# First routing of a two-layer expert kernel: another layout of the list values, and another order of the work around it

## The chip, the cores and the metric

One core of one Trainium2 chip runs the whole program. The metric is the device time of one execution in microseconds (us). Besides TensorE (PE; PEld is its weight load), VectorE (DVE), ScalarE (ACT) and GpSimd (POOL), SP issues most of the DMAs, and POOL issues the gathers and scatters.

## The reference

The input goes through a 2-D Fourier transform (real part), then through a first layer of 8 experts weighted by a Sinkhorn iteration over all tokens, then through a second layer in which each token goes to one expert only:

```
X = fft(fft(x, axis=1), axis=2).real            # x: 8 x 3072 x 256
x = X.reshape(24576, 256)
logits = x @ w_gate;  logits -= logits.max()
P = exp(logits)
for _ in range(8):
    P /= P.sum(1, keepdims=True) + 1e-9
    P /= P.sum(0, keepdims=True) + 1e-9
    P *= N / E
out = sum over e of P[:, e:e+1] * (relu(x @ w1[e]) @ w2[e])          # first layer
# second layer: logits = out @ w_gate2, the row's best expert alone, scaled by its softmax weight
```

The exponentials of the first layer are zero for most rows and experts, so only the few rows that count are routed to experts.

## The kernel before

**Stages.** The transform writes rows to a DRAM table `H` and logits to an SBUF tile `L`. Then `route1` finds which rows and experts matter, and makes for each of `NT1` = 29 tiles (128 rows each: three per expert for 8 experts, and five "free" ones) the list of rows. `moe1` gathers those rows from `H`, builds inputs from them (`build`, four steps a to d), turns them with TensorE transposes (`turn`) and runs the experts one after the other. `route2` and `moe2` do the same for the second layer. The order of instructions on each engine is the order of the program text; work that belongs beside other work is put in by hand through `hooks` and `Slots` (a slot is a place between the groups of matmuls of an expert).

**The list products (`route1`).** Each partition holds `NSA` = 64 slots. `oh` (29 tiles x 64 slots, bf16) marks the tile of each slot, `bv` holds two values per tile and slot (`v` = 0: the row's column `ja`; `v` = 1: the partition's number), and `ah` marks the row within the tile (128 rows x n slots, made by `rows` in the chunks `CH1` = 24, 24 and 16). `put` then issues one matmul per slot, 64 in all, which add up in one PSUM tile `pl`: weights `ah[:, :, i]` (128 x 128, elements 48 or 32 bytes apart) and values `bv[:, :, :, a + i]` (58 columns, 128 bytes apart, since the slot is the innermost dimension of `bv`). From `pl` DVE works out `j`, and from that `R["hidx"]`, the rows to gather; then `signs` prepares further masks and a second product (`bq`, 24 matmuls of 16 columns with the first chunk's `ah`) into a tile of the pool `py`.

**What fills the engines meanwhile.** `G2` is a string for each hook of `route1`: `g` is one half of an expert's small weight product (`gates2`, half-gate; 16 matmul records with `wg2`), `0` to `3` make the high part (`part`) of a piece of expert 0's weights on ACT and put its low part (a DVE subtraction) on a list, `l` and `z` issue DMAs (a copy of `L`, zero fills of `out` and `acc`), `w` is one matmul of zeros (`warm`). `hooks[3]` comes between `bv` and the matmuls of `put`, `hooks[4]` behind them: there `low(0)` runs both low parts of expert 0's w1 on DVE and then fetches the next weights. After the first two groups of gathers, `fill(5)` issues the last half-gates.

**Weight loads.** `FETCH` is the order of the loads and their buffers: `("t", 7, "a")` is the last expert's transposed w2, which the half-gates of expert 7 need. It goes to buffer `rawa`, which expert 0's w1 occupies until `low(0)` is done. Buffers "1" and "2" are tiles of the pools that hold the experts' split weights. `gates2` fetches the next load behind experts 0, 1, 2 and 7.

**Into expert 0.** In `moe1`, `build(0, V, i)` makes the three input tiles of expert 0 on DVE as their gathers land; `moe.turn` transposes them in six matmuls, with a hook behind each pair that issues two 512-column matmuls of zeros (`lambda i: warm(2)`) from the pool `py`, which has two buffers; then the first layer's matmuls (`ph`) begin. `rest[3]` in slot (0, 0) runs the two low parts of expert 0's w2.

Of the kernel before, what the change touches and what calls it, by code (L numbers as in the profile page):

```python
# [7 lines left out]
F32 = mybir.dt.float32  # L8
F32R = mybir.dt.float32r
BF16 = mybir.dt.bfloat16  # L10
# [8 lines left out]
HW = 281  # L19
# [542 lines left out]


def route1(nc, rt, L, rmx, K, R, keep, pool, ring, hooks):
    o = rt.o
# [92 lines left out]
    oh = rt.tiles(T, tb, NSA)  # L658
    bv = T([2, NT1, NSA], BF16, name="bv")
    o.tt(bv[:, 0], oh, ja[:, None, :].to_broadcast([128, NT1, NSA]), ALU.mult)  # L660
    nc.scalar.activation(out=bv[:, 1, :, :NSL], in_=oh[:, :, :NSL], func=AF.Copy, scale=C("p"))
    nc.scalar.activation(out=bv[:, 1, :, NSL:], in_=oh[:, :, NSL:], func=AF.Copy, scale=C("p128"))
    hooks[3]()
# [3 lines left out]
    for n in CH1:  # L667
        a = NSL if a is None else a % NSA
        ah = rt.rows(ring, rb, a, n)
        late = late or ah  # L670
        rt.put(pl, ah, bv, a, n, a == NSL, a + n == NSL)
        a += n
    eq, gq = T([8, NSL], name="eq"), T([8], name="gq")
    o.tt(eq, ja[:, NSL:NSL + 8, None].to_broadcast([128, 8, NSL]), ja[:, None, :NSL].to_broadcast([128, 8, NSL]), ALU.is_equal)
    o.tt(eq, eq, gp[:, None, :NSL].to_broadcast([128, 8, NSL]), ALU.mult)
    hooks[4]()
    lst, li = S([2, NT1], name="lst"), T([NT1], I32, name="li")
# [10 lines left out]
    def signs():  # L688
# [8 lines left out]
        o.stt(R["ow"], R["hidx"], 2.0, sb, ALU.mult, ALU.add)  # L697

        o.red(gq, eq, ALU.add)
        tq, rq, _ = rt.split(T, gq, None, 8, "q")  # L700
# [334 lines left out]
def dense(tc, ctx, A, K, rt, R, Ld, H, Pd, out, wg2):  # L1035
# [69 lines left out]
    with tc.For_i(0, NT, 1) as i:  # L1105
# [17 lines left out]
        for s in range(2):  # L1123
# [26 lines left out]
FETCH = [("t", 0, "a"), ("t", 1, "b"), ("t", 2, "c"), ("t", 3, "1"), ("t", 4, "2"), ("t", 5, "2"), ("w1", 0, "a"), ("w2", 0, "b"),  # L1150
         ("t", 6, "c"), ("t", 7, "a"), ("w1", 1, "a"), ("w2", 1, "b")]
FETCH += [(w, e, b) for e in range(2, E) for w, b in (("w1", "a"), ("w2", "b"))]
# [4 lines left out]
def run(tc, ctx, A, out, H, acc, Ld, Pd, Gd, Zd):  # L1157
# [62 lines left out]
    with tc.manual_schedule():  # L1220
# [27 lines left out]
        with ExitStack() as st:  # L1248
# [7 lines left out]
            def gates2(e, qs=(0, 1)):  # L1256
# [15 lines left out]
                raw.pop(("t", e))  # L1272
                if e < 3 or e == E - 1:
                    fetch()
# [24 lines left out]
            with ExitStack() as s1:  # L1299
# [15 lines left out]
                def fill(k):  # L1315

                    def f():
                        for c in G2[k]:
# [5 lines left out]
                            elif c == "z":  # L1324
# [4 lines left out]
                                for a in range(0, n, 512):  # L1329
                                    w = min(512, n - a)  # L1330
                                    nc.sync.dma_start(out=av[:, a:a + w], in_=zt[:, 0, :w])
                            elif c == "w":
                                warm(1)
                            else:
                                part("w", 0, int(c), nc.vector, lows[int(c) // 2])
# [3 lines left out]
                def low(k):  # L1339
                    for f in lows[k]:  # L1340
                        f()

                signs, later = route1(nc, rt, L, rmx, K, R, S, r1, ring, [fill(i) for i in range(1, 5)] + [lambda: low(0)])
                X = {}

# [18 lines left out]
            with ExitStack() as s1:  # L1364
# [16 lines left out]

                turned, more = moe1(nc, K, R, rt, lg, hot, acc, moe, W, part, X, xg, Gd, *rows("w1", "w2"), xb, pt, zeros, zt, later[:2] + (rest, lambda: low(1), grab), ask, rt.C("tro"), lambda i: warm(2), lambda: xg.tile([128, CAP, HW], F32, name="Xg").rearrange("p a b -> p (a b)")[:8, :512])
            with ExitStack() as s1:
# [92 lines left out]
BACK, BF, BL = [(8,), (8,), (8,), (8,), (4, 8), (2, 4, 6, 8)], ((2, 9), (4, 9), (6, 9)), 8  # L1476
G2 = ("gg", "", "gggggg", "0lz12g3gg", "ggww", "ggg")
Y2 = (2, 3, 9, 10)
# [114 lines left out]
def moe1(nc, K, R, rt, lg, hot, acc, moe, W, part, X, xg, Gd, w1f, w2f, xb, pt, zeros, zt, rest, ask, trash, warm, grow):  # L1593
# [116 lines left out]
    for i in range(CAP):  # L1710
        for f in build(0, V, i):
            f()
    xt = moe.turn(lambda i: x[0][:, i], warm)
    for i, f in zip((0, 1, 3, 4), (rest[3], rest[0], rest[1], begin)):
        sl.at(0, i, f)
# [146 lines left out]
```

## Time and profile before

| | |
|---|---|
| median of 3 runs | 662.18 us (656.67, 662.18, 663.15) |
| profiled execution, its own time | 660.44 us |
| its span, first to last instruction | 658.7 us |
| mean granted TensorE clock | 0.97 |
| PE busy | 627.1 us (95%), 4794 matmuls |
| PEld busy | 600.1 us (91%) |
| DVE busy | 442.6 us (67%) |
| ACT busy | 321.6 us (49%) |
| POOL busy | 194.6 us (30%) |

All rows come from this one execution; times are us from the start of its span. The routing and the way into expert 0 lie between 197 and 249 us. Matmuls are pipelined, so a busy PE there is not PE at its peak: the spacing of the instructions and the granted clock say more.

### The profile page before, as it was taken

To read this page: it belongs to the slowest core of one execution; us is meant where nothing else is said; L and a number is where in the kernel's file an instruction comes from. 1 tells how busy PE (TensorE), PEld (TensorE's weight loads), DVE (VectorE), ACT (ScalarE), POOL (GpSimd) and SP (SyncE) were. 2 spreads that over 40 slices of the span, in tenths; PEclk is the share of its full clock that TensorE was granted. 3 is DMA by queue.
4 is the path that set the end of the run, shared out by engine and by line. 5 is a ranking of instruction groups with operands and counts; after the bars stand their busy time and mean duration, and the time that the engine had idled before them with its cause. 6 is when DMAs were issued, how large, how long until landed. Compare 5 with 4: busy or idle time off the path is not lost. (4 is left out here: it accounts for less than half of the span.)

```text
span 658.7 us, 12655 instructions
## 1 busy us (share of the span) xinstructions
PE 627.1 (95%) x4794; PEld 600.1 (91%) x4794; DVE 442.6 (67%) x1019; ACT 321.6 (49%) x717; POOL 194.6 (30%) x325
## 2 busy tenths in 40 slices
PE   9999999999998989999999998997999999999985
PEld 6899999999998968999999988984899999999984
DVE  4697787777238948659898789664555664674570
ACT  3455555555544204657556555531455564574441
POOL 0002221022110078831201102123686654431331
PEclk9999999999999879999999999998899999999988
DMA  8999999999979765676766758992565547635500
GB/s 222 285 234 323 279 274 280 260 301 308 343 256 374 300 192 177 199 269 206 258 206 218 281 179 229 307 374 44 176 214 194 205 148 296 237 138 210 208 33 29
DMA packets 56785, 152.58 MB, mean 232 GB/s; under 512 B 8292, under 2 KB 25836, under 8 KB 49165
## 3 DMA queue, kind: packets, MB, share of 16 engines
q1 hardware_dynamic: 47500, 114.69, 54.4%
q0 software_dynamic: 8752, 36.50, 17.0%
q8 instruction: 40, 0.66, 0.4%
q10 hardware_dynamic: 464, 0.51, 0.2%
q14 instruction: 29, 0.23, 0.1%
HBM read 101.50 MB, written 50.07 MB: 230 GB/s over the span
## 5 line engine op out<-in xcount | busy, mean ns | idle before, releaser
L933 PE MATMUL py<-w2h,hh 128*128 128x256 f32 (+1 forms) x472 | 137.0, 290 | 1.4 <-ACT y L1655 1.4
L436 DVE SCALAR_TENSOR_TENSOR hl<-ph,hh 128x384 fp32r<-128x384 f32 (+1 forms) x161 | 84.6, 542 | 78.1 <-ACT hh L886 75.8
L933 PE MATMUL py<-w2l,hh 128*128 128x256 f32 (+1 forms) x472 | 134.5, 285 | 2.3 <-DVE w2l L836 2.0
L933 PE MATMUL py<-w2h,hl 128*128 128x256 f32 (+1 forms) x472 | 134.9, 286 | 1.3 <-DVE hl L436 1.0
L886 ACT ACTIVATE hh<-ph 128x384 fp32r<-128x384 f32 (+1 forms) x161 | 75.8, 481 | 60.4 <-PE ph L900 32.7
L933 PEld LDWEIGHTS py<-w2l,hh 128*128 128x128 f32 x472 | 90.3, 191 | 2.7 <-DVE w2l L836 2.2
L933 PEld LDWEIGHTS py<-w2h,hl 128*128 128x128 f32 x472 | 90.1, 191 | 2.1 <-DVE hl L436 1.6
L933 PEld LDWEIGHTS py<-w2h,hh 128*128 128x128 f32 x472 | 90.1, 191 | 1.8 <-ACT y L1655 1.6
L900 PE MATMUL ph<-xh,w1h 128*128 128x384 f32 x256 | 68.2, 348 | 4.3 <-DVE hl L436 3.8
L900 PE MATMUL ph<-xh,w1l 128*128 128x384 f32 x256 | 65.3, 336 | 0.0
L900 PE MATMUL ph<-xl,w1h 128*128 128x384 f32 x256 | 65.3, 336 | 0.0
L74 PE MATMUL pp<-ca,w 96*128 96x96 f32 x512 | 59.0, 275 | 0.0
L74 PEld LDWEIGHTS pp<-ca,w 96*128 96x128 f32 x512 | 58.2, 192 | 0.5 <-ACT Z L97 0.2
L807 POOL DMA_INDIRECT out_dram<-y,Rorow x30 | 31.8, 1062 | 89.5 <-ACT hh L886 37.8
L126 POOL TENSOR_TENSOR lc<-hd 128x32 f32<-128x32 f32 (+1 forms) x25 | 9.5, 380 | 164.4 <-ACT hd L122 149.4
L900 PEld LDWEIGHTS ph<-xh,w1h 128*128 128x128 f32 x256 | 45.0, 189 | 7.6 <-DVE hl L436 6.0
L84 DVE COPY t<-pp 128x512 f32<-128x512 f32 (+2 forms) x56 | 33.3, 608 | 24.2 <-PE pp L82 24.2
L91 PE MATMUL pp<-cb,t 128*128 128x128 f32 x368 | 47.5, 276 | 0.6 <-DVE t L84 0.6
L900 PEld LDWEIGHTS ph<-xh,w1l 128*128 128x128 f32 x256 | 46.5, 189 | 0.0
L900 PEld LDWEIGHTS ph<-xl,w1h 128*128 128x128 f32 x256 | 46.3, 188 | 0.0
L76 ACT ACTIVATE at<-pp 128x384 f32<-128x384 f32 x64 | 31.1, 491 | 30.6 <-PE pp L74 30.1
L91 PEld LDWEIGHTS pp<-cb,t 128*128 128x128 f32 x368 | 44.4, 192 | 0.9 <-DVE t L84 0.8
(346 smaller groups left out, 1262.9 us busy)
## 6 DMA issues: line engine op xcount, KB each, us to landing
out_dram<-zt SPq DMA_DIRECT2D x48, 512.0 KB
H<-hd SPq DMA_DIRECT2D x24, 562.0 KB
xa<-in_xa_dram SPq DMA_DIRECT2D x32, 384.0 KB
xm<-in_xm_dram SPq DMA_DIRECT2D x32, 384.0 KB
rawa<-in_w_dram SPq DMA_DIRECT2D x8, 1024.0 KB
rawb<-in_w_dram SPq DMA_DIRECT2D x8, 1024.0 KB
rawa<-in_u_dram SPq DMA_DIRECT2D x8, 1024.0 KB
rawb<-in_u_dram SPq DMA_DIRECT2D x8, 1024.0 KB
```

The costliest lines, as they stand in the source:

```text
L74: nc.tensor.matmul(p[:M, i], lhs(4 * h + i), ca, start=True, stop=True)
L76: nc.scalar.activation(out=at[:M, :, :, s0:s0 + 4], in_=p[:M].rearrange("m s g j -> m g j s"), func=AF.Copy)
L84: nc.vector.tensor_copy(out=t[:, :n, :M], in_=p[:, :n, :M])
L91: nc.tensor.matmul(p[:M, i * 128:(i + 1) * 128], t[:, i, :M], cb[:, (g0 + i) * 128:(g0 + i + 1) * 128], start=True, stop=True)
L126: nc.gpsimd.tensor_tensor(out=lc[:np_, :n], in0=hd[:np_, :, 129:137], in1=hd[:np_, :, 273:281], op=ALU.add)
L436: self.nc.vector.scalar_tensor_tensor(out, a, s, b, op0, op1)
L807: nc.gpsimd.indirect_dma_start(out=dst, out_offset=bass.IndirectOffsetOnAxis(ap=idx, axis=0), in_=src, in_offset=None, **kw)
L886: self.nc.scalar.activation(out=a[:, :n], in_=p[:, :n], func=AF.Relu)
L900: self.nc.tensor.matmul(p[:, :N], w, xx, start=(i == 0), stop=(i == 5))
L933: self.nc.tensor.matmul(p[:, :nd], c, W[2 + m // 4][w][:, m % 4, :nd], start=(m == 0 and i == 0), stop=(m == 7 and i == 2))
```

## The change

- `bv` is laid slot by slot: for each slot its 58 values stand side by side. DVE and ACT write it through a transposed view. A new function `packed` takes the place of `put` for the first product: the 58 values of a slot are read contiguously and streamed twice (116 columns; the second copy lands in columns of `pl` that nobody reads).
- Expert 7's w2 (`t`, 7) goes to a buffer of pool "1" and is fetched behind expert 3's half-gates, not behind `low(0)`.
- `G2`: one half-gate moves ahead of the positions, one ahead of the products; the two zero matmuls `ww` become five `v`, each of two 512-column matmuls of zeros in the pool `ph`.
- `low(0)` at `hooks[4]` runs only its first low part; the second, and the fetch behind it, run after the builds of expert 0, before `turn`. The two `eq` operations move from before `hooks[4]` into `signs`.
- `turn` no longer gets matmuls of zeros in its hook.

```diff
+    def packed(self, pl, ah, bv, a, n, first, last):
+        nv = bv.shape[2]
+        for i in range(n):
+            self.nc.tensor.matmul(pl[:, :2 * nv].rearrange("p (k v) -> p k v", k=2), ah[:, :, i], bv[:, a + i, None].to_broadcast([128, 2, nv]),
+                                  start=first and i == 0, stop=last and i == n - 1)
...
-    bv = T([2, NT1, NSA], BF16, name="bv")
-    o.tt(bv[:, 0], oh, ja[:, None, :].to_broadcast([128, NT1, NSA]), ALU.mult)
-    nc.scalar.activation(out=bv[:, 1, :, :NSL], in_=oh[:, :, :NSL], func=AF.Copy, scale=C("p"))
-    nc.scalar.activation(out=bv[:, 1, :, NSL:], in_=oh[:, :, NSL:], func=AF.Copy, scale=C("p128"))
+    bv = T([NSA, 2 * NT1], BF16, name="bv")
+    tv = bv.rearrange("p n (v t) -> p v t n", v=2)
+    o.tt(tv[:, 0], oh, ja[:, None, :].to_broadcast([128, NT1, NSA]), ALU.mult)
+    nc.scalar.activation(out=tv[:, 1, :, :NSL], in_=oh[:, :, :NSL], func=AF.Copy, scale=C("p"))
+    nc.scalar.activation(out=tv[:, 1, :, NSL:], in_=oh[:, :, NSL:], func=AF.Copy, scale=C("p128"))
...
-        rt.put(pl, ah, bv, a, n, a == NSL, a + n == NSL)
+        rt.packed(pl, ah, bv, a, n, a == NSL, a + n == NSL)
...
+    hooks[4]()
...
-    o.tt(eq, ja[:, NSL:NSL + 8, None].to_broadcast([128, 8, NSL]), ja[:, None, :NSL].to_broadcast([128, 8, NSL]), ALU.is_equal)
-    o.tt(eq, eq, gp[:, None, :NSL].to_broadcast([128, 8, NSL]), ALU.mult)
-    hooks[4]()
...
+        o.tt(eq, ja[:, NSL:NSL + 8, None].to_broadcast([128, 8, NSL]), ja[:, None, :NSL].to_broadcast([128, 8, NSL]), ALU.is_equal)
+        o.tt(eq, eq, gp[:, None, :NSL].to_broadcast([128, 8, NSL]), ALU.mult)
...
-         ("t", 6, "c"), ("t", 7, "a"), ("w1", 1, "a"), ("w2", 1, "b")]
+         ("t", 6, "c"), ("t", 7, "1"), ("w1", 1, "a"), ("w2", 1, "b")]
...
-                if e < 3 or e == E - 1:
+                if e < 4:
...
-                            elif c == "w":
-                                warm(1)
+                            elif c == "v":
+                                p = ph.tile([128, 512], F32, name="ph")
+                                for _ in range(2):
+                                    nc.tensor.matmul(p, zb[:, :128], zb, start=True, stop=True)
...
-                signs, later = route1(nc, rt, L, rmx, K, R, S, r1, ring, [fill(i) for i in range(1, 5)] + [lambda: low(0)])
+                    lows[k].clear()
...
+                signs, later = route1(nc, rt, L, rmx, K, R, S, r1, ring, [fill(i) for i in range(1, 5)] + [lambda: lows[0].pop(0)()])
...
-                turned, more = moe1(nc, K, R, rt, lg, hot, acc, moe, W, part, X, xg, Gd, *rows("w1", "w2"), xb, pt, zeros, zt, later[:2] + (rest, lambda: low(1), grab), ask, rt.C("tro"), lambda i: warm(2), lambda: xg.tile([128, CAP, HW], F32, name="Xg").rearrange("p a b -> p (a b)")[:8, :512])
+                turned, more = moe1(nc, K, R, rt, lg, hot, acc, moe, W, part, X, xg, Gd, *rows("w1", "w2"), xb, pt, zeros, zt, later[:2] + (rest, low, grab), ask, rt.C("tro"), lambda i: None, lambda: xg.tile([128, CAP, HW], F32, name="Xg").rearrange("p a b -> p (a b)")[:8, :512])
...
-G2 = ("gg", "", "gggggg", "0lz12g3gg", "ggww", "ggg")
+G2 = ("gg", "", "ggggggg", "0lz12g3gg", "ggvvvvv", "gg")
...
+    rest[3](0)
...
-    for i, f in zip((0, 1, 3, 4), (rest[3], rest[0], rest[1], begin)):
+    for i, f in zip((0, 1, 3, 4), (lambda: rest[3](1), rest[0], rest[1], begin)):
```

## Rows read from the trace of the kernel before

**Rows 1.** The page: busy us of an engine, share, instructions.

```profile
PE   627.1 (95%) x4794; PEld 600.1 (91%) x4794; DVE 442.6 (67%) x1019; ACT 321.6 (49%) x717; POOL 194.6 (30%) x325
```

**Rows 2.** Timeline around the products: start us, us, engine, line, operation, count [idle before].

```profile
220.76 1.12 DVE L427 TENSOR_TENSOR bv<-oh,ja 128x1856 bf16<-128x1856 bf16 x1
...
221.80 4.56 DVE L427 TENSOR_TENSOR ah<-irx,rba 128x3072 bf16<-128x3072 bf16 x3
221.98 0.86 ACT L662 ACTIVATE bv<-oh,cst 128x696 bf16<-128x696 bf16 x1
...
222.97 0.59 PE L1282 MATMUL py<-zb 128*128 128x512 bf16 x2 [0.36 <-ACT g L1265]
...
223.61 6.73 PEld L560 LDWEIGHTS <-ah 128*128 128x128 bf16 x64 [0.54 <-DVE ah L427]
...
226.79 0.49 DVE L427 TENSOR_TENSOR eq<-eq,gsa 128x320 f32<-128x320 f32 x1
227.20 2.35 DVE L836 TENSOR_TENSOR w1l<-rawa,w1h 128x1024 fp32r<-128x1024 f32 x2
229.58 0.33 SPq L1217 DMA_DIRECT2D rawa<-in_w2t_dram  x1
...
230.39 3.65 PE L1263 MATMUL py<-wg,rawc 128*128 128x96 f32 x16
230.60 0.19 DVE L433 TENSOR_SCALAR j<-pt 128x29 int32<-128x29 f32 x1 [1.05 <-PE pt L560]
```

**Rows 3.** Windows: stretch, length, PE, PEld, DVE, ACT, POOL busy, clock, DMA share, GB/s.

```profile
209.50:211.50 2.00, 0.17 (x2) 0.06 (x1) 1.83 (x11) 0.46 (x2) 0.00 (x0) 1.00 0.96 397
...
223.60:226.00 2.40, 2.39 (x23) 2.39 (x24) 2.40 (x2) 0.00 (x0) 0.00 (x0) 1.00 1.02 386
226.00:228.00 2.00, 2.00 (x21) 2.00 (x20) 1.97 (x4) 0.00 (x0) 0.00 (x0) 0.79 0.23 75
228.00:230.40 2.40, 2.40 (x26) 2.40 (x24) 1.56 (x2) 0.00 (x0) 0.00 (x0) 0.50 0.00 0
...
247.00:248.00 1.00, 1.00 (x6) 1.00 (x5) 0.54 (x2) 0.00 (x0) 1.00 (x2) 0.69 1.01 308
```

**Rows 4.** Timeline from the lists to expert 0's first matmuls.

```profile
231.62 1.13 POOL L802 DMA_INDIRECT Xg<-H,Rhidx  x1 [34.87 <-DVE sb L431]
...
234.31 0.95 POOL L802 DMA_INDIRECT Xg<-H,Rhidx  x1 [0.30 <-issue]
...
234.97 3.78 PE L1263 MATMUL py<-wg,rawa 128*128 128x96 f32 x32 [0.93 <-DMA rawa<-in_w2t_dram]
235.22 0.30 DVE L1602 TENSOR_TENSOR Xg<-Xg 128x33 f32<-128x33 f32 x2 [0.32 <-DMA Xg<-H,Rhidx]
...
238.48 1.51 PEld L560 LDWEIGHTS <-ah 128*128 128x128 bf16 x20
...
239.15 0.30 DVE L1602 TENSOR_TENSOR Xg<-Xg 128x33 f32<-128x33 f32 x2 [1.96 <-DMA Xg<-H,Rhidx]
...
241.74 0.93 PE L853 MATMUL pt<-ident,x 128*128 128x128 f32 x2
...
245.54 0.63 PE L853 MATMUL pt<-ident,x 128*128 128x128 f32 x2
...
246.54 1.13 PE L900 MATMUL ph<-xh,w1h 128*128 128x384 f32 x2
...
248.96 0.56 DVE L436 SCALAR_TENSOR_TENSOR hl<-ph,hh 128x384 fp32r<-128x384 f32 x1 [1.42 <-issue]
```

**Rows 5.** Timeline of DVE in the second routing: two operations of one size.

```profile
439.18 0.40 DVE L427 TENSOR_TENSOR rk<-rk,w 128x232 f32<-128x232 f32 x1
...
440.27 0.60 DVE L427 TENSOR_TENSOR M<-rk,kp 128x232 f32<-128x232 f32 x1
```

**Rows 6.** Timeline of POOL, then of ACT: the first free tile's w2.

```profile
279.10 0.94 POOL L802 DMA_INDIRECT rawc<-in_w_dram,Rfrow  x1 [0.30 <-issue]
...
293.33 1.05 ACT L830 ACTIVATE w2h<-rawc 128x1024 fp32r<-128x1024 f32 x1
```

## Prediction

> **What bounds the kernel now.** I read the page's busy times first: PE is busy for 627.1 of 658.7 us [rows 1]. A change that adds no speed to a matmul can then only gain where PE waits or idles in disguise. So I looked at the stretch that the diff touches, first by its timeline, then by windows with the granted clock. Three things are to be seen there. First, the products: DVE makes `bv` and the three `ah`, the 64 matmuls start when the first `ah` is there (223.61) and run 6.73 us, 105 ns each, and DVE waits for them before `j` at 230.60 [rows 2]. Their pace does not come from the clock: 24 weight loads fit into 2.40 us at granted clock 1.00, and 24 into 2.40 us at 0.50 [rows 3]. Second, expert 7's half-gates wait for their load until 234.97; behind them in PE's order stand the `bq` product (238.48) and the six transposes [rows 4]. Third, the transposes: the first pair runs at 241.74, the last at 245.54, with matmuls of zeros between, though the last input tile was ready near 240.2 (it starts at 239.15 and takes 1.0 us like the others). The first layer's matmuls begin at 246.54, DVE's first `hl` at 248.96 [rows 4]. From there PE is nearly always busy, so I forecast the shift of these two instants and ask what gives it back.
>
> **Values laid slot by slot, cost on DVE.** `bv` took 1.12 us for 1856 bf16 values [rows 2]. Its write now steps 58 values of 2 bytes, 116 bytes. No row of the trace writes bf16 so. The nearest row writes f32 with that very step: `M`, 232 values, 29 x 4 = 116 bytes apart, took 0.60 us where `rk` of the same size, contiguous, took 0.40 [rows 5]. With 320 values in 0.49 us [rows 2] a contiguous f32 value costs 0.09/88 = 1.02 ns over a base of 0.16; the stride adds 0.20/232 = 0.86. So 1856 values cost 0.16 + 1856 x 1.88 = 3.65 us, 2.5 more than before. The other end is no change (1.12); one value per 1.02 ns with no stride cost would be 2.06. I take 3.65, since its row has the step. ACT writes the other half beside it, done at 222.84 before [rows 2]; even with 0.86 ns more per value it ends at 224.4, before the first `ah` does, so it costs nothing. The first matmul moves from 223.61 to 226.1.
>
> The Trainium skill ("VectorE: DVE Perf Modes", "What auto-detection actually checks") says that two results per cycle need 16-bit tensors that all have step one. It speaks against the new layout. The rule alone, with no further cost of a stride, would lead to the 2.06 us above. The rows agree that more than this can be lost, as `M` is f32 and still slower by half.
>
> **The same, gain on PE.** 105 ns per slot with 58 columns at either clock means that reading binds, of the weights or of the values. The `bq` product reads weights of the same `ah` with only 16 columns: 20 loads in 1.51 us, 75 ns [rows 4]. So strided weights alone allow 75 ns, and the strided values made it 105. Contiguous values need at most their columns: 512 columns take 0.59/2 = 0.30 us or less [rows 2], so 116 take at most 67 ns at the high clock; hidden under 75. I take 75 ns: 64 x 75 = 4.8 us instead of 6.73. Bounds: 105 (the weights bind after all) and, with the columns at the low clock, at most 2 x 67 = 134 ns. DVE's two later chunks come 1.75 and 2.97 us behind the first (4.56 us for all three [rows 2]) and just keep up. So `j` moves to 226.1 + 4.8 + 0.3 = 231.2, 0.6 later than now.
>
> The Trainium skill ("TensorE: Matmul & The Clock Gate", "Step-by-step: what each phase is for") gives TensorE two independent read ports, one for weights and one for the moving operand. Then the slower of the two sets the pace, 75 ns here. The rows 105 and 75 fit that, but they also fit two reads that take turns, which is a rival below.
>
> **Zero matmuls and half-gates ahead.** PE idles from 209.6 to 211.4 [rows 3]; one half-gate (3.78/2 = 1.9 us [rows 4]) fits there and costs nothing, because DVE leads until the products. The five remaining end near 221.6 (at the high clock) and the ten `v` at 0.30 or less end by 224.6, before 226.1. If `bv` were cheap they would cost up to 1.0. They should keep the clock from falling, which it did inside the old product: 0.79, then 0.50 [rows 3].
>
> **Last w2 sooner.** It goes to SP's queue directly behind expert 6's load, ahead of the copy of `L` and the zero fills, which move back by one load: 1 MB at 386 GB/s [rows 3], 2.7 us. The queue is empty from 228 now, so it would be empty near 230; the first gather starts at 231.62 + 0.6. Nobody waits for the fills soon. PE no longer waits: after the products it has two half-gates, 3.8 us (7.3 at the low clock, 3.65 each [rows 2]), until 234.8, instead of three and a wait until 238.5.
>
> **The chain from `j`.** Now 230.60 to the first build at 235.22, of which 0.32 is a wait for the gather: 4.30 us of small DVE work [rows 2, 4]. `eq` (twice 0.49 [rows 2]) moves from the cover of the product onto this path: +0.98. So the first build begins at 231.2 + 5.3 = 236.5, three builds end at 239.5. The third gather, issued at 234.31, landed at 239.15, 4.84 later; the first took 3.6 [rows 4]. With 0.6 more it lands between 238.5 and 239.8, so the builds end between 239.5 and 240.8; I take 240.0. On PE `bq` starts with the first build and takes 3.3 us until the first transposes (238.48 to 241.74, stalls included [rows 4]): 239.8, hidden.
>
> **Transposes without zeros, and the low part.** From the last pair to the first `ph` it took 1.0 us [rows 4]; with 0.2 to start, `ph` begins at 241.2 instead of 246.54, 5.3 earlier. The low part moved behind the builds (half of 2.35, 1.2 us [rows 2]) runs while PE transposes and ACT copies, and the first matmul that needs it is the fourth; cost 0, at most 1.2 without that cover. The load of expert 1's w1 behind it is issued near 241, 1 us sooner than now (behind the last half-gates), so nothing is late there.
>
> **Clock at the start.** PE does little from 235 on, and without the zeros it should start the first layer at the low level (1.2 of 2.4 GHz); before, the window 247 to 248 had 0.69 already [rows 3]. The 2.42 us from `ph` to `hl` become about 2.8: +0.4. Afterwards DVE, not PE, leads for some 10 us, so more low clock costs little.
>
> **Sum.** -5.3 + 0.4 = -4.9 us. Against the profiled execution's own 660.44 that is 655.5. The median, 662.18, lies 1.7 above it, and the three runs lie 6.5 us apart, so about 1% is what a measurement of this kernel can tell from no change. I forecast 656.
>
> **Rivals.**
> - *`bv` is cheap.* At 2.06 us all moves 1.6 earlier (653.9), at 1.12 some 2.5 less the 1.0 that the zeros then cost (654). With luck in the gathers 652.5. For it: the strided row is f32, not bf16. Against it: the same byte step. Chance 0.25.
> - *The weights bind.* The product stays at 105 ns: 64 x 30 ns = 1.9 us back, 657.4. For it: `ah` keeps its strides. Against it: `bq` at 75. Chance 0.15.
> - *Given back at the free tiles.* POOL issues its gathers in one long row that starts with `hidx`, so it starts 0.6 later and not 4.9 earlier. The first free tile's w2 is issued at 279.10 and used at 293.33 [rows 6]; used at 288.4, with an issue at 279.7, 8.7 us are left. If its landing takes 11, ACT waits 2.3: 657.8. Chance 0.12.
> - *Slower: reads take turns.* [...] With the half-gates at the low level `ph` comes 12.6 behind `j`, so this decides from a `j` at 233.5 on, or 111 ns per slot. Against it: no row shows a bf16 pair so slow. Chance 0.05.
> - *As forecast*, 653.5 to 657.5: 0.43.
>
> **Range.** From 652 (cheap `bv`) to 660.5 (weights that bind, with the low clock under the half-gates: `j` at 233.2, `ph` at 245.8); it leaves out the slower case and the ends. Faster by over 1% needs 6.6 us: most of the cheap `bv` and a tail of the forecast, 0.28. Slower by over 1% needs more than the slow rival gives: 0.03. Within 1%: 0.69.
>
> **What would show it.** `bv` near 3.65 us; 64 loads with 116 columns in about 4.8 us at clock 1.00; no wait for the last w2; `j` near 231.2; no zeros between the transposes; `ph` near 241.2 and `hl` near 244. The forecast is wrong if `bv` keeps its 1.12, if the loads stay at 105 ns, if the third gather comes later than the second build, or if the lead of 5 us at `hl` is no longer there behind expert 2.

## The result, and the profile after

The changed kernel took 665.16 us (median of 17 runs, 660.13 to 667.55); the kernel before, run beside it, 659.68 us (17 runs, 652.85 to 663.15). The ratio is 1.008, its 95% interval 1.0058 to 1.0102: 5.3 us slower, where 4.9 us faster was forecast. Where a gain or a loss is told "by the ratio", it is the ratio's share of the time; the difference of two medians can lie some 1 us beside it. The profiled execution took 662.54 us, its span 660.7.

PE's busy time on the page hardly moved [rows 1]; DVE has 7 us more.

```profile
PE 623.3 (94%) x4796; PEld 597.9 (90%) x4796; DVE 449.4 (68%) x1019; ACT 328.4 (50%) x717; POOL 194.8 (29%) x325
```

The instant at which `bv` starts differs from execution to execution (220.76 in the first profile of before [rows 2], 224.63 here, between 221.5 and 226.8 in all later ones), for a reason ahead of the change: the windows 40 to 50 and 50 to 60 us have a granted clock of 1.00 where it starts early and of 0.72 to 0.91 where it starts late, in the kernel before as well. So all instants below are told **behind the start of `bv`**; the expectations count from the start of `oh`, 1.15 us sooner.

The timeline of the changed kernel from `bv` to the first layer, then the first free tile's w2, answers [rows 2, 4, 6]:

```profile
224.63 8.46 DVE L427 TENSOR_TENSOR bv<-oh,ja 128x1856 bf16<-128x1856 bf16 x1
224.68 5.48 ACT L669 ACTIVATE bv<-oh,cst 128x1160 bf16<-128x1160 bf16 x1 [3.16 <-DVE oh L427]
224.69 2.32 PE L1343 MATMUL ph<-zb 128*128 128x512 bf16 x10
229.65 3.58 ACT L670 ACTIVATE bv<-oh,cst 128x696 bf16<-128x696 bf16 x1
232.69 4.78 DVE L427 TENSOR_TENSOR ah<-irx,rba 128x3072 bf16<-128x3072 bf16 x3
...
234.72 5.35 PE L567 MATMUL pt<-bv,ah 128*128 128x116 bf16 x64 [7.71 <-DVE ah L427]
...
240.11 0.19 DVE L433 TENSOR_SCALAR j<-pt 128x29 int32<-128x29 f32 x1 [1.51 <-PE pt L567]
...
241.13 1.13 POOL L810 DMA_INDIRECT Xg<-H,Rhidx  x1 [40.38 <-DVE sb L431]
...
245.49 0.28 DVE L1613 TENSOR_TENSOR Xg<-Xg 128x33 f32<-128x33 f32 x2
...
248.02 0.29 DVE L1613 TENSOR_TENSOR Xg<-Xg 128x33 f32<-128x33 f32 x2 [0.53 <-DMA Xg<-H,Rhidx]
...
248.90 0.69 PE L861 MATMUL pt<-ident,x 128*128 128x128 f32 x2 [1.03 <-DVE x L1613]
...
249.95 1.07 PE L908 MATMUL ph<-xh,w1h 128*128 128x384 f32 x2 [0.37 <-ACT xh L864]
...
252.87 0.56 DVE L436 SCALAR_TENSOR_TENSOR hl<-ph,hh 128x384 fp32r<-128x384 f32 x1 [1.75 <-ACT hh L894]
...
291.16 0.94 POOL L810 DMA_INDIRECT rawc<-in_w_dram,Rfrow  x1 [0.30 <-issue]
...
297.46 1.06 ACT L838 ACTIVATE w2h<-rawc 128x1024 fp32r<-128x1024 f32 x1 [1.58 <-DMA rawc<-in_w_dram,Rfrow]
...
301.64 0.62 PE L908 MATMUL ph<-xh,w1h 128*128 128x384 f32 x2 [2.12 <-DVE hl L436]
```

The reader sees four things. `bv` took 8.46 us on DVE, where it took 1.12, and 8.55 us on ACT (224.68 to 233.23), where the two parts had taken 2.0 (220.81 to 222.84). PE then stood idle for 7.71 us, until the first `ah`, which stands behind `bv` on DVE. So `j` came 15.48 us behind the start of `bv` (240.11 - 224.63) instead of 9.84 [rows 2]. From `j` on the chain is shorter by nearly as much: `ph` starts 9.84 behind `j`, against 15.94 [rows 2, 4], so that `hl` comes 28.24 behind `bv` against 28.20. Lastly, POOL's row of gathers starts with the lists, so `rawc` is issued 66.5 us behind `bv` (58.3 before [rows 6]); ACT waits for it, and DVE has `w2l` ahead of the next `hl`, for which PE waits 2.12 us.

The windows of the products, with the granted clock in the column behind POOL, answer [rows 3]:

```profile
226.00:228.00 2.00, 1.01 (x5) 0.28 (x3) 2.00 (x1) 2.00 (x1) 0.00 (x0) 1.00 1.05 408
228.00:230.40 2.40, 0.00 (x0) 0.00 (x0) 2.40 (x1) 2.40 (x2) 0.00 (x0) 1.00 1.05 407
...
234.00:236.00 2.00, 1.27 (x14) 1.28 (x15) 2.00 (x2) 0.00 (x0) 0.00 (x0) 0.50 0.01 3
236.00:238.00 2.00, 2.00 (x26) 2.00 (x24) 2.00 (x3) 0.00 (x0) 0.00 (x0) 0.58 0.00 0
238.00:240.00 2.00, 2.00 (x32) 2.00 (x32) 0.60 (x1) 0.00 (x0) 0.00 (x0) 1.00 0.00 0
```

After its idle stretch PE met the product at the lower level (0.50), and came back to 1.00 only within it. At 1.00 a slot costs less than the forecast's 75 ns: 26 of them take 1.90 us, 73 ns each at most.

```profile
237.90 1.90 PE L567 MATMUL pt<-bv,ah 128*128 128x116 bf16 x26
```

### The profile page after: what moved, and what is told of

The parts are those of the page before. It is cut to its first block, busy times and chain, and to the rows that moved or that the text cites. A ratio compares the mean times of both kernels' runs of the same rounds, so it can differ in the third digit from the quotient of the medians.

```text
span 660.7 us, 12661 instructions
## 1 busy us (share of the span) xinstructions
PE 623.3 (94%) x4796; PEld 597.9 (90%) x4796; DVE 449.4 (68%) x1019; ACT 328.4 (50%) x717; POOL 194.8 (29%) x325
## 5 line engine op out<-in xcount | busy, mean ns | idle before, releaser
L941 PE MATMUL py<-w2h,hl 128*128 128x256 f32 (+1 forms) x472 | 133.5, 283 | 0.8 <-DVE hl L436 0.8
L908 PE MATMUL ph<-xl,w1h 128*128 128x384 f32 x256 | 66.5, 342 | 0.0
L74 PE MATMUL pp<-ca,w 96*128 96x96 f32 x512 | 60.6, 279 | 0.3 <-DVE w L160 0.3
L74 PEld LDWEIGHTS pp<-ca,w 96*128 96x128 f32 x512 | 59.6, 196 | 1.0 <-issue 0.5
L84 DVE COPY t<-pp 128x512 f32<-128x512 f32 (+2 forms) x56 | 33.3, 608 | 23.3 <-PE pp L82 23.3
L151 DVE TENSOR_TENSOR xa<-xa,xm 96x1024 f32<-96x1024 f32 x32 | 38.9, 1214 | 9.9 <-DMA xm<-in_xm_dram 9.9
```

Source lines behind the costliest of these rows:

```text
L74: nc.tensor.matmul(p[:M, i], lhs(4 * h + i), ca, start=True, stop=True)
L84: nc.vector.tensor_copy(out=t[:, :n, :M], in_=p[:, :n, :M])
L151: e.tensor_tensor(out=xa[:, c], in0=xa[:, c], in1=xm[:, c], op=ALU.add)
L908: self.nc.tensor.matmul(p[:, :N], w, xx, start=(i == 0), stop=(i == 5))
L941: self.nc.tensor.matmul(p[:, :nd], c, W[2 + m // 4][w][:, m % 4, :nd], start=(m == 0 and i == 0), stop=(m == 7 and i == 2))
```

## The experiments

My theory after the result: the write of `bv` costs all of the loss, and the rest of the change gains some us. Rivals: ACT and DVE slow each other down, writing one tile together; the new product or the rest of the change loses too; the loss arises later, at the free tiles. The table has the instants of every run that was timed, in us behind the start of `bv` (the run with everything contiguous is charged the 0.97 us that its `oh` takes longer); "turn" is from the transposes of expert 2's input to those of expert 3's. Ratios are to runs of the kernel before on the same chip.

| run | `bv` DVE | `j` | `ph` | `hl` | turn | ratio (95%) |
|---|---|---|---|---|---|---|
| before, first profile | 1.12 | 9.84 | 25.78 | 28.20 | 19.1 | |
| before again | 1.13 | 9.88 | 23.92 | 26.00 | 19.5 | 1.000 (0.997 to 1.003) |
| changed | 8.46 | 15.48 | 25.32 | 28.24 | 22.4 | 1.008 (1.006 to 1.010) |
| changed again | 8.48 | 16.41 | 26.25 | 29.16 | 20.3 | 1.008 (1.004 to 1.012) |
| layout alone | 8.45 | 15.94 | 31.53 | 33.61 | 19.1 | 1.009 (1.005 to 1.013) |
| old layout | 1.13 | 9.86 | 23.81 | 26.71 | 19.1 | 0.995 (0.992 to 0.998) |
| one writer | 8.38 + 4.64 | 20.35 | 32.37 | 35.28 | 22.7 | 668.66 us, one run |
| all contiguous | 2.10 | 10.30 | 22.87 | 25.77 | 19.4 | 0.997 (0.993 to 1.001) |
| swapped loops | 3.54 | 10.77 | 20.11 | 23.02 | 20.8 | 0.999 (0.995 to 1.002) |
| rows early | 8.46 | 16.38 | 26.25 | 29.16 | 19.1 | 1.006 (1.003 to 1.010) |
| old, rows early | 1.12 | 9.86 | 19.22 | 22.13 | 19.1 | 0.996 (0.993 to 0.999) |
| swapped, rows early | 3.54 | 10.84 | 20.50 | 23.41 | 19.1 | 0.996 (0.993 to 0.999) |
| old, zeros back | 1.12 | 9.84 | 20.31 | 22.40 | 20.3 | 0.993 (0.991 to 0.996) |
| old, zeros, rows early | 1.13 | 9.87 | 19.88 | 21.97 | 19.1 | 0.990 (0.985 to 0.994) |
| swapped, zeros, rows early | 3.53 | 10.79 | 20.84 | 22.92 | 19.1 | 0.992 (0.988 to 0.995) |

**1. Old layout in the changed kernel** (`e1_old_layout`): `bv` and the product as before, all else as changed.

```diff
-    bv = T([NSA, 2 * NT1], BF16, name="bv")
-    tv = bv.rearrange("p n (v t) -> p v t n", v=2)
+    bv = T([2, NT1, NSA], BF16, name="bv")
...
-        rt.packed(pl, ah, bv, a, n, a == NSL, a + n == NSL)
+        rt.put(pl, ah, bv, a, n, a == NSL, a + n == NSL)
```

> The changed kernel with the list values and the first product as before (58 strided columns, DVE and ACT write contiguously); all other parts of the change stay. Theory 1 (the writes with a step of 116 bytes are the loss): bv takes 1.1 us on DVE instead of 8.46, the 64 matmuls some 6.7 us instead of 5.2, j comes about 11 us behind the start of oh instead of 16.6, the first layer's matmuls about 21 us behind it instead of 26.5, ACT does not wait for the first free tile's w2 in expert 2, and the time is 654 to 657 us, under the kernel before (660). Rival (the other parts of the change cost, or the transform does): the time stays at 662 or more.

657.16 us against 661.68, by the ratio 3.3 us faster than the kernel before. So the rest of the change gains, and the layout loses more than that. But `ph` came 13.95 us behind `j`, and not 9.84, by a wait that the timeline shows:

```profile
241.72 0.86 PE L860 MATMUL pt<-ident,x 128*128 128x128 f32 x6
...
246.92 0.87 ACT L863 ACTIVATE xh<-pt 128x384 fp32r<-128x384 f32 x2 [6.41 <-remote]
```

PE's rows have all six transposes done by 242.58; ACT, which waits for PE alone, got PE's signal 4.3 us later ("remote": the profile has no instruction that ends where the signal came). I come back to this below.

**2. The layout alone in the kernel before** (`e2_layout_only`): the same lines, put into before.

> The kernel before with the layout of the list values and the packed product alone. Theory 1: bv takes 8.5 us, j comes 16 to 17 us behind oh, the first layer's matmuls 32 us behind it (26.9 before), and the time is 665 to 669 us, longer than the whole change (665), since nothing pays for it. Rival: within 2 us of the kernel before.

666.34 us against 661.68, by the ratio 5.8 us slower. The layout alone loses as much as the whole change; that the rest pays 3.3 us without the new layout (run 1) and only some 0.5 with it (this run against the changed kernel) lies within the intervals.

**3. One writer** (`e3_one_writer`): DVE writes all of `bv`, ACT none.

```diff
-    nc.scalar.activation(out=tv[:, 1, :, :NSL], in_=oh[:, :, :NSL], func=AF.Copy, scale=C("p"))
-    nc.scalar.activation(out=tv[:, 1, :, NSL:], in_=oh[:, :, NSL:], func=AF.Copy, scale=C("p128"))
+    o.ts(tv[:, 1, :, :NSL], oh[:, :, :NSL], C("p"), ALU.mult)
+    o.ts(tv[:, 1, :, NSL:], oh[:, :, NSL:], C("p128"), ALU.mult)
```

> The changed kernel, but DVE alone writes all of the list values; ACT writes none, so the two engines no longer write the same tile at the same time. If two writers get into each other's way, DVE's first part (1856 values) falls from 8.46 us to about 3.7, the price of the strided f32 row, and the whole of it takes some 7.4 us. If the 2-byte writes with the step are slow by themselves, the first part stays near 8.4 us, and the other two parts add as much again, so the products start some 8 us later than in the changed kernel.

```profile
226.10 8.38 DVE L427 TENSOR_TENSOR bv<-oh,ja 128x1856 bf16<-128x1856 bf16 x1
234.10 4.64 DVE L431 TENSOR_SCALAR bv<-oh,cst 128x1160 bf16<-128x1160 bf16 x2
```

With ACT silent DVE's first write took 8.38 us, as with ACT beside it (8.46): ACT does not slow this write, and this rival falls. The other two writes (1160 and 696 values) took 3.05 and 1.99 us, far less per value than the expectation had; run 13 comes back to that.

**4. All contiguous** (`e4_all_contig`): `oh` is made slot by slot as well, so that every read and write runs through memory in order, and the product stays packed.

```diff
-    oh = rt.tiles(T, tb, NSA)
+    oh = T([NSA, NT1], BF16, name="oh")
+    o.tt(oh, K["itx"], tb[:, :, None].to_broadcast([128, NSA, NT1]), ALU.is_equal)
...
+    bv = T([NSA, 2, NT1], BF16, name="bv")
+    o.tt(bv[:, :, 0], oh, ja[:, :, None].to_broadcast([128, NSA, NT1]), ALU.mult)
```

> The changed kernel, but the marks oh are also made slot by slot, so that DVE and ACT read and write everything contiguously (the operand that is spread over the tiles has step zero instead of one). Theory 1: oh and bv take about 2.1 us each (one value per 1.02 ns over 0.16), ACT 1.3 and 0.9 us, the 64 matmuls 5.2 us; j comes about 11.5 us behind oh, and the time is 654 to 658 us, like the version with the old layout. Rival (the loss is elsewhere): 662 or more.

The same tile in memory, the same product, and the loss is gone: 658.87 against 661.68. `oh` and `bv` take 2.08 and 2.10 us, 1.13 ns a value instead of 0.60; in both the smaller operand now repeats along the inner loop, but no run varies that alone. ACT's wait for PE's signal is here too, 2.7 us.

**5. The changed kernel again** (`e5_after_again`), on another chip.

> The changed kernel, unaltered, profiled and timed a second time beside the next runs. In its first profile the first layer's matmuls began 9.84 us behind j, while in the runs with the old layout and with everything contiguous ACT's copies of the transposes came 3 to 4 us later than PE's rows end, so that they began 13.95 and 12.57 us behind j. Theory 'the delay is common, and the first profile of the changed kernel happened to lack it': here the first layer begins 11.5 to 14 us behind j. Rival 'the delay belongs to the fast layouts': again 9.8 us. Either way bv takes 8.4 us, the product 5.3 us, j comes 16.6 us behind the start of oh, and the time is 664 to 667 us.

`ph` came 9.84 us behind `j` again, with no late signal: the rival held for this run, but see run 10. The product took 6.24 us, at a granted clock of 0.50 up to its last microsecond (0.72 from 239 to 240):

```profile
233.70 6.24 PE L567 MATMUL pt<-bv,ah 128*128 128x116 bf16 x64 [7.74 <-DVE ah L427]
```

That is 97 ns a slot. The changed kernel's ten matmuls of zeros start 0.216 us apart at 1.00, 0.42 ns for each of 512 columns; at half the clock 116 columns would take 98 ns. So at the low level the columns bind, by this estimate.

**6. Rows early** (`e6_rows_early`): the first free tile's w2 and gate rows gathered behind its w1.

```diff
-        sl.at(F1 + f - 1, FREE["w"][1], lambda f=f: free.weights(f, (1, 2)))
+        sl.at(F1 + f - 1, FREE["w"][1 if f else 0], lambda f=f: free.weights(f, (1, 2)))
```

> The changed kernel with the gathers of the first free tile's w2 and of its gate rows issued right behind that of its w1, two groups of token gathers sooner (about 11 us). Theory 'a part of the loss is given back at the first free tile, because POOL's row of gathers starts 5.6 us later': expert 2's turn, which took 22.4 us in the changed kernel and 19.1 us in the kernels without the late row, takes 19.1 us again, w2h no longer waits for rawc, and the time falls by 3 us, to 661 to 663. Rival 'PE has slack there': the turn may shorten, but what comes behind is bound by other work and the time stays within 1 us of the changed kernel's.

The turn fell from 20.3 to 19.1 us, and `w2h` waits for `rawc` no more. By the ratios the time is 0.9 us less than that of run 5 on the same chip, but the intervals overlap: the wait is shown, its price in the time is not.

**7. Swapped loops** (`e7_swapped_loops`): the same tile, but the write walks it in memory's order, and `oh` is read with a step of 128 bytes.

```diff
-    tv = bv.rearrange("p n (v t) -> p v t n", v=2)
-    o.tt(tv[:, 0], oh, ja[:, None, :].to_broadcast([128, NT1, NSA]), ALU.mult)
+    tv = bv.rearrange("p n (v t) -> p v n t", v=2)
+    ot = oh.rearrange("p t n -> p n t")
+    o.tt(tv[:, 0], ot, ja[:, :, None].to_broadcast([128, NSA, NT1]), ALU.mult)
```

> The changed kernel, with the same tile of values, slot by slot, and the same product, but bv's writes walk it in the order of its memory and read oh with a step of 128 bytes instead. Theory 'what costs is the write in steps of 116 bytes': DVE's part takes about 2 us (one value per 1.04 ns and a start), ACT's parts 1.3 and 0.9 us, j comes 10 to 11 us behind oh instead of 16.6, and the time is 657 to 659 us. Rival 'any walk in steps of over 100 bytes costs 4.5 ns a value, on the read side too': the parts take 8 and 5.5 us as before and the time stays at 665.

```profile
221.49 3.54 DVE L427 TENSOR_TENSOR bv<-oh,ja 128x1856 bf16<-128x1856 bf16 x1
...
226.74 5.48 PE L567 MATMUL pt<-bv,ah 128*128 128x116 bf16 x64 [2.87 <-DVE ah L427]
```

The theory had some 2 us for the write and the rival 8: `bv` took 3.54 us, `j` came at 10.77, `hl` at 23.02. The prediction's own sum had 3.65, 10.44 and 23.3. This is the kernel that I had predicted, and its time is 656.22 us; but the kernel before took 656.49 on this chip. Against the changed kernel on this chip (run 5) the walk of the write alone is worth 6.0 us by the ratios, whose intervals lie apart. Against the second profile of before (run 9) the lead is 3.0 us at `hl`, 1.6 at the transposes of expert 3 and 1.3 at the end: the turn of expert 2, 20.8 us, gives a part of it back.

**8. Prices of the write** (`e8_prices`): extra writes of `oh`'s values into `bv`'s memory ahead of its own, which are overwritten.

```diff
+    v116 = fl.rearrange("p (n v t) -> p v t n", v=2, t=NT1)
+    v64 = fl[:, :2048].rearrange("p (n t) -> p t n", t=32)
...
+    o.tt(v116[:, 0], oh, jb(NT1, NSA), ALU.mult)
+    o.tt(v64[:, :NT1], oh, jb(NT1, NSA), ALU.mult)
```

> The changed kernel with the old layout of bv, and ahead of bv's own writes thirteen extra instructions that write oh's values into bv's memory in other patterns, and are overwritten; only the durations of these instructions are of interest, and the time (some 60 us longer) is not. On DVE, one after the other with ACT idle: products of two bf16 operands written with steps of 116 bytes, contiguous but read with a step, with steps of 128, 64, 32, 16 and 4 bytes, as f32 with a step of 116 bytes; then a product with a constant at 116 bytes. On ACT with DVE idle: 116 bytes, contiguous but read with a step, f32 at 116 bytes, contiguous. Theory 'a 2-byte value written alone costs more than a 4-byte one, wherever it lands': all steps over 4 bytes cost 3 to 4.5 ns a value, f32 at 116 bytes 1.9 ns. Rival 'the price is of the distance': it falls with the step, to near 1 ns at 16 bytes. ACT alone at 116 bytes: 4.7 ns a value if the price is the engine's own, 2.5 or less if it had been slowed by DVE beside it.

The timeline, DVE in the order of the expectation's list, then ACT:

```profile
223.52 8.38 DVE L427 TENSOR_TENSOR bv<-oh,ja 128x1856 bf16<-128x1856 bf16 x1
231.93 3.27 DVE L427 TENSOR_TENSOR bv<-oh,ja 128x1856 bf16<-128x1856 bf16 x1
235.24 7.64 DVE L427 TENSOR_TENSOR bv<-oh,ja 128x1682 bf16<-128x1682 bf16 x1
242.91 8.21 DVE L427 TENSOR_TENSOR bv<-oh,ja 128x1856 bf16<-128x1856 bf16 x1
251.16 4.44 DVE L427 TENSOR_TENSOR bv<-oh,ja 128x1024 bf16<-128x1024 bf16 x1
255.63 2.42 DVE L427 TENSOR_TENSOR bv<-oh,ja 128x512 bf16<-128x512 bf16 x1
258.08 2.21 DVE L427 TENSOR_TENSOR bv<-oh,ja 128x1856 bf16<-128x1856 bf16 x1
260.33 3.47 DVE L427 TENSOR_TENSOR bv<-oh,ja 128x1856 f32<-128x1856 bf16 x1
263.83 8.35 DVE L431 TENSOR_SCALAR bv<-oh 128x1856 bf16<-128x1856 bf16 x1
...
272.27 8.49 ACT L687 ACTIVATE bv<-oh,cst 128x1856 bf16<-128x1856 bf16 x1 [51.85 <-DVE bv L431]
280.79 3.42 ACT L688 ACTIVATE bv<-oh,cst 128x1856 bf16<-128x1856 bf16 x1
284.24 3.60 ACT L689 ACTIVATE bv<-oh,cst 128x1856 f32<-128x1856 bf16 x1
287.88 1.84 ACT L690 ACTIVATE bv<-oh,cst 128x1856 bf16<-128x1856 bf16 x1
```

Divided by their values: 4.51 ns at 116 bytes, 4.54 at 128, 4.42 at 64, 4.34 at 32, 4.73 at 16 (few values, so the start weighs more), 1.19 at 4 bytes, 0.60 contiguous (1.12 us). Read with a step but written in order: 1.76. As f32 at the same 116 bytes: 1.87. ACT pays the same: 4.57 ns alone at 116 bytes, 1.94 as f32, 1.84 with the step on the read side, 0.99 in order. So the theory held: the price is of a 2-byte value that lands alone, and it is no matter how far the next one lies from 16 bytes on. Nor is it the DMA traffic beside it: the first write ran while the queues moved 382 GB/s, the last one on DVE while they moved nothing, in 8.38 and 8.35 us. The Trainium skill ("SBUF — State Buffer", "Specifications (TRN2)") gives lines of 16 bytes and a penalty for each access that crosses to a new one. The steps of 16 to 128 bytes agree with that, while a step of 8 bytes, two values to a line, is not cheap either (2.39 ns in run 13); it gives no price, and by the line alone the f32 row would cost as much as the bf16 row.

**9. The kernel before again** (`e9_before_again`).

> The kernel before, unaltered, profiled a second time beside the next runs: a ratio of 1.00, whatever the theory. What it is for: in its first profile the half-gates of expert 7, the bq product and the zeros were signalled up to 1 us later than PE's rows end, and the first layer began 26.93 us behind the start of oh. Theory 'the first profile caught it late, by a delay that the runs of some chips show and others do not': here the first layer begins 24.5 to 26 us behind oh. Rival 'the first profile is typical': 26.5 to 27.5 us.

The instants of the theory "caught late" came true: the first layer began 25.07 us behind `oh`. The timeline of this second profile:

```profile
225.91 1.13 DVE L427 TENSOR_TENSOR bv<-oh,ja 128x1856 bf16<-128x1856 bf16 x1
...
235.79 0.19 DVE L433 TENSOR_SCALAR j<-pt 128x29 int32<-128x29 f32 x1 [1.08 <-PE pt L560]
...
249.83 0.83 PE L900 MATMUL ph<-xh,w1h 128*128 128x384 f32 x2
...
251.91 0.56 DVE L436 SCALAR_TENSOR_TENSOR hl<-ph,hh 128x384 fp32r<-128x384 f32 x1 [1.08 <-ACT hh L886]
```

`hl` comes 26.00 behind `bv`, against 28.20 in [rows 2, 4], with `j` at the same place: 2.2 us of what I had counted as the change's to win were not there in this execution. From its `bq` matmuls to `ph` PE took 7.95 us in the first profile (238.59 to 246.54, at a granted clock of 0.50 from 242 to 246) and 3.81 us in the second (246.02 to 249.83, at 1.00 from 247 on); expert 7's half-gates took 3.78 us in the first and 6.34 in the second. So the clock lay at another level in either, and that late signals alone made the difference is not shown. Against this profile the changed kernel's `hl` is 2.2 us late (3.2 in its second profile), and its end, 436.1 and 435.2 behind `bv` against 430.9, 5.2 and 4.3: the measured 5.3.

**10. Old layout, rows early** (`e10_old_rows_early`): runs 1 and 6 together.

> The changed kernel with bv laid and streamed as before, and with the first free tile's w2 and gate rows gathered right behind its w1. Theory 'the rest of the change is worth some us, and only the new layout loses': 0.3 to 0.8% faster than before, as without the earlier gathers, since expert 2 did not wait in that kernel; the two token groups that now come 2.5 us later are not waited for. Rival 'the token groups 6 and 7 are due': a wait of up to 2.5 us at the logits or the later inputs, and no gain over before.

655.20 against 657.69. `ph` came 9.36 us behind `j`, so run 1's late signal is no part of that version: the same instructions up to there show it in one execution and not in another.

```profile
243.98 0.85 PE L860 MATMUL pt<-ident,x 128*128 128x128 f32 x6
...
244.76 0.87 ACT L863 ACTIVATE xh<-pt 128x384 fp32r<-128x384 f32 x2 [2.00 <-PE pt L860]
...
245.30 1.07 PE L907 MATMUL ph<-xh,w1h 128*128 128x384 f32 x2 [0.47 <-ACT xh L863]
```

**11. Swapped loops, rows early** (`e11_swapped_rows_early`): runs 7 and 6 together.

> The changed kernel with bv's writes in the order of its memory (reads stepped) and the earlier gathers. In the run with the swapped walk alone, the first layer began 21.3 us behind oh (26.9 before), but expert 2's turn took 20.8 us instead of 19.1. Theory 'that wait for w2 is the last thing that gives the lead back': the turn takes 19.1 us, and the time is 1.5 us under that of the swapped walk alone, 0.2 to 0.5% under before. Rival 'the lead is given back elsewhere as well': within 0.1% of before.

A ratio of 0.996, where run 7 had 0.999; the turn took 19.1 us instead of 20.8. Its interval reaches to 0.9989, that of run 7 from 0.9949: the gain of the earlier rows is not settled by the time alone.

**12. Old layout, zeros back** (`e12_old_zeros_back`): run 1 with the matmuls of zeros behind the transposes.

```diff
-rt.C("tro"), lambda i: None,
+rt.C("tro"), lambda i: warm(2),
```

> The changed kernel with bv laid and streamed as before, and with the two matmuls of zeros put back behind each pair of transposes. Theory 'without the zeros the first layer begins about 1 us sooner and then pays for the low clock': the first layer begins 1 us later behind j than without zeros, at a granted clock nearer 1.0, and the time is within 1 us of that without zeros. Rival 'the zeros were worth their time, the clock decides': 1 to 2 us faster with them. Rival 'the zeros were what delayed the start': 3 us slower with them.

652.62 against 657.69. `ph` begins 1.09 us later than without zeros (run 10), but `hl` follows it by 2.09 instead of 2.91 us, at a granted clock of 1.00 (0.50 in run 10's window from 246 to 248): at `hl` the two differ by 0.27 us. The median is 2.6 us below run 10's 655.20 on the same chip, although run 10 has the earlier gathers as well; but the intervals overlap, so the first theory ("within 1 us") and the rival ("1 to 2 us faster") are not told apart.

**13. More prices** (`e13_prices2`).

```diff
+    o.ts(v116[:, 1], oh, C("p"), ALU.mult)
+    o.ts(v116[:, 1, :, :NSL], oh[:, :, :NSL], C("p"), ALU.mult)
+    o.tt(v116[:, 0, :, :NSL], oh[:, :, :NSL], jb(NT1, NSL), ALU.mult)
...
+    for k in range(14):
+        o.cp(v2[:, k], o2[:, k])
```

> As the first run of prices: the changed kernel with the old layout of bv and, ahead of bv's own writes, extra writes of oh's values into bv's memory that are overwritten; only their durations count. On DVE: the product at a step of 116 bytes into the second half (58 bytes off), a product with a constant there, products with a pointer scalar into the first and the second half, the same into 40 slots of the second half (which took 3.05 us in the run where DVE wrote both halves), the product of two operands into 40 slots, a copy into the first half, the product with a step of 8 bytes (896 values), and copies of two neighbouring values at each step of 116 bytes (14 copies of 128 values). Theory 'one price for every 2-byte value that lands alone': 4.4 to 4.6 ns a value everywhere, the 3.05 us remain odd, and the 128 values of a pair copy take about 0.3 us (64 steps of 4.5 ns). Rival 'the pointer scalar halves it': 2.6 ns a value in the three writes with C(p) alone. Rival 'the short walk halves it': 2.6 ns in both writes into 40 slots.

The timeline, of the product with a pointer scalar into all slots, the same into 40, the product of two operands into 40, the one with a step of 8 bytes, and the first two copies of neighbouring pairs:

```profile
249.24 8.57 DVE L431 TENSOR_SCALAR bv<-oh,cst 128x1856 bf16<-128x1856 bf16 x1
257.84 2.87 DVE L431 TENSOR_SCALAR bv<-oh,cst 128x1160 bf16<-128x1160 bf16 x1
260.31 5.50 DVE L427 TENSOR_TENSOR bv<-oh,ja 128x1160 bf16<-128x1160 bf16 x1
...
274.23 2.14 DVE L427 TENSOR_TENSOR bv<-oh,ja 128x896 bf16<-128x896 bf16 x1
276.41 0.23 DVE L439 COPY bv<-oh 128x128 bf16<-128x128 bf16 x1
276.55 0.22 DVE L439 COPY bv<-oh 128x128 bf16<-128x128 bf16 x1
```

Neither the theory nor a rival held as put. All walks over all slots cost 4.50 to 4.62 ns a value, whichever half and scalar; into 40 slots two operands still cost 4.74, and one operand 2.47. What the cheap one has, and the others lack, is both one operand only and the same counts on both sides (40 by 29; over all slots the read side is one run of 1856). The Trainium skill ("VectorE: DVE Perf Modes", "What auto-detection actually checks") lets an operation with one source take two results at a time when the outermost counts of source and destination are equal or both even; here they are 29 and 29, against 1856 and 29 over all slots, and the 2.47 against 4.62 agrees with that, as do the writes into 40 and 24 slots of run 3 (2.63 and 2.86 ns). A step of 8 bytes cost 2.39 ns a value. The copies of pairs follow each other by 0.14 us: 64 steps, 2.2 ns for two neighbouring values. These copies have one operand and equal counts on both sides too, and there one value alone cost 2.47: a pair costs about as much as a single value.

**14 and 15. The zeros, with old and with swapped layout, rows early** (`e14_old_zeros_rows`, `e15_swapped_zeros_rows`).

> The changed kernel with the old layout and product, the zeros back between the transposes, and the first free tile's rows gathered early. Theory 'what the runs so far pay adds up': expert 2's turn 19.1 us instead of the 20.3 with zeros alone, and 0.7 to 0.9% faster than before. Rival 'given back': 0.4 to 0.7%, as either alone.

> The same with the new layout and the slot-by-slot product, written in the order of its memory. Theory 'the product's gain of 1.5 us is eaten by the dearer write even when it is walked well': j comes 1 us later than with the old layout (11.9 against 11.0 us behind oh) and the time is 0 to 1 us longer. Rival 'the columns keep the clock up and the first layer gains': 1 us shorter.

651.67 and 652.61 against 658.99. Run 14 has the lowest ratio of all, 0.9895, a little more gain than its theory had; against run 15 the intervals overlap. Written well, the slot-by-slot product has 1.43 us less on PE (5.52 against 6.95 in run 12), but `bv` costs 2.4 more ahead of it, and `j` comes 0.9 later, as the theory had it.

## Why the prediction was wrong, step by step

**The step that failed is the cost of `bv` on DVE.** I sized 1856 values at 1.88 ns from the row of `M` [rows 5], which has the same byte step, but writes 4 bytes: 3.65 us. It was 8.46. For 4-byte values the working was right (3.47 us in run 8); 2-byte values that land alone cost 2.4 times as much (8.38). The same tile written in the order of its memory took 3.54 us and 6.0 us less in all (run 7). I had noted that no row writes bf16 so, and then took the row's price for the upper end as well; its 3.65 was no bound. ACT's half, "costs nothing", ended 8.6 us behind `bv`, not 3.6 as I had it; DVE's wait hid it.

**The product** was a second term that was mis-sized, by 0.6 to 1.4 us: 5.35 us (84 ns a slot), 6.24 in run 5 and 5.48 (86) in runs 4 and 7, not 4.8. The size of a slot was not the error, as at 1.00 it took 73 ns at most; the clock was. The prediction let the ten matmuls of zeros keep it up. They ended at 227.0, PE idled for 7.71 us, and the product began at 0.50. With the `bv` of the sum (run 7) PE still idled for 2.87 us, and the clock was 0.69 on average over the product. In the kernel before it fell within the product with PE busy all the time [rows 3], so that the idle stretch brings the low clock is not shown. The first matmul came 10.09 us behind `bv` instead of 5.3, and `j` 5.0 later than predicted.

**From `j` on the sum held in the changed kernel.** First build 5.38 us behind `j` (predicted 5.3), the third build waiting 0.53 us for its gather (predicted: the gather ends last), the last pair of transposes to `ph` 1.05 (1.0), no wait for the last w2, the low part hidden behind transposes and copies, and `ph` to `hl` 2.92 us at the low clock (2.8). So `ph` came 4.9 us later than predicted, which is the 5.0 of `j`. Run 7, where `bv` did cost 3.54, has the predicted `j` and `hl` within 0.35 us.

**The base was off as well.** The sum was made against a profile whose `hl` came 2.2 us later than that of the second profile of before (run 9). With the right `bv` the change would thus have gained 2.7 us and not 4.9 at the first layer; in time it is 0.9 us by the ratio of run 7, whose interval, 3.4 us faster to 1.4 slower, leaves out 4.9. Of the 10.2 us between forecast and result, the walk of the write is 6.0 and the base 2.2; the other 2 lie within the intervals, with 1.3 seen in the turn of expert 2 in run 7 (20.8 us against 19.5).

**Rivals.** "Given back at the free tiles" came true beside the failed step: expert 2's turn took 22.4 and 20.3 us instead of 19.5, with the wait for `rawc` that the rival names, and issuing the rows earlier took it away. "Slower: reads take turns" had the right side by a wrong mechanism: the product took 84 to 97 ns a slot on average, under the 111 that it named, and at 1.00 no more than the 75 of `bq`; `j` passed the instant that it named (12.7 behind `bv`) because DVE wrote slowly, and the half-gates then ran at 1.00, not at the low clock, so `ph` came 9.84 behind `j` and not 12.6. The rule of the Trainium skill that I weighed ("VectorE: DVE Perf Modes", "What auto-detection actually checks") spoke against the layout rightly; the sum by the rule alone, 2.06 us, was further off than mine.

**What stays open**: what holds PE's signals back in runs 1, 3 and 4, where ACT got them 2 to 4 us behind PE's rows. The three come from one chip and one batch, but run 2 of that batch, and runs 14 and 15 on that chip later, do not show it, and neither do runs 5 to 7 and 9 to 12 on two others: so it is not a matter of the chip alone. Also open is whether the zeros between the transposes gain time (run 12 against 10, on one chip, with overlapping intervals).

## What to carry to other kernels

Price a new access by a row with the same width of value, the same side (write or read) and the same step; where none exists, the next width is not a bound. If a tile must change its order, let the write run in memory's order and put the step on the reads, here 1.76 ns a value instead of 4.51 (1.91 with ACT writing beside it). Profile the kernel before a second time, ahead of the sum: here one execution was late by 2.2 us in the very stretch that the change was about.

## What the runs showed of the hardware

- A bf16 value written alone cost 4.3 to 4.7 ns on DVE at steps of 16, 32, 64, 116 and 128 bytes, and 4.6 on ACT at 116; on DVE 2.4 at 8 bytes and 1.2 at 4; f32 at 116 bytes 1.9 on both. DVE, writing the tile beside ACT, was not slowed (8.46 against 8.38 us); ACT took 4.7 to 5.1 ns a value beside DVE and 4.57 alone.
- With one operand and equal counts on both sides DVE wrote such values at 2.47 ns (run 13).
- Weights of `ah` with 116 streamed columns: 97 ns a slot at a granted clock of 0.50, 84 to 86 partly at 1.00, at most 73 at 1.00 throughout.
- ACT got PE's signal up to 4.3 us behind the ends that PE's rows show in runs 1, 3 and 4, and at once in runs 2, 5 to 7, 9 to 12, 14 and 15; runs 1 and 10 have the same instructions up to there.
